# Block 0 of an attention-and-GLU kernel listed anew: eight raw buffers, own buffers for batch 0, some steps on GpSimd

## The chip, the cores and the metric

One core of one Trainium2 chip. The time is that of one execution on the device in microseconds (us); the kernel before was run three times. A profiled execution on the same kind of core gives the rows. Engines in the rows: PE is TensorE (matmul), PEld its weight loads, DVE is VectorE, ACT is ScalarE, POOL is GpSimd, SP is SyncE, whose queue issues most loads. A q behind the name (SPq) is the engine's instruction queue.

## What is computed

Attention over 8 batches, 8 heads, 576 positions and 64 columns, then a gated layer over all 4608 tokens.

```python
scores = scale * np.matmul(q, k.transpose(0, 1, 3, 2))
mask_local = (rel >= 0) & (rel < stride)                                   # heads 0 to 3, stride 32
mask_strided = (rel >= 0) & (pos[None, :] % stride == pos[:, None] % stride)  # heads 4 to 7
attn = np.exp(scores - max); attn = attn / (sum + 1e-09); x = attn @ v
gate = 1.0 / (1.0 + np.exp(-(x @ w_gate)))
out = (gate * (x @ w_val)) @ w_out         # x: 4608 x 512, w_gate and w_val: 512 x 1536, w_out: 1536 x 512
```

A query sees at most 32 keys in the local heads and 18 in the strided ones, and the kernel computes only the blocks that hold them.

## The kernel before

**Pieces.** A piece is a pair of heads of one batch, 32 in all: pieces 0 and 2 of a batch are local, 1 and 3 strided. Its steps: Q and V load queries with keys, and values (L261, L265); S scores on TensorE (L295); F masks them out of PSUM (L310, L315), takes the row maximum (L319) and subtracts it (L323), all on VectorE; E is the exponential on ScalarE (L334); N the row sum, its small corrections and the product with its reciprocal on VectorE (L338 to L344); T transposes on TensorE (L355, L359), P copies the result out on ScalarE (L376, L378); X weighs the values on TensorE (L399). The result is split in two float32r parts, high by ScalarE (H, L435) and low by VectorE (L, L439), and the last 64 tokens of the batch are kept apart (R, L448). Each piece gives one 128-row quarter of the 512-wide x of its batch.

**Blocks.** The gated layer goes over nine blocks of 512 tokens: block k is the first 512 tokens of batch k, block 8 the rests. For each of twelve f (128 columns of the hidden layer) a block has a gate product g, a value product v and an output product O or o, each of twelve 128x128x512 matmuls (three per quarter of x: high by high, high by low, low by high; L478, L509). Between them stand sigmoid s (ScalarE, L486), gating m (VectorE, L491), and the split of the hidden part, high x (ScalarE, L498) and low y (VectorE, L502). From block 3 on two blocks at a time take sums of weights out of DRAM (L762), which saves products; those sums are made on GpSimd during blocks 1 and 2 (L685, L690).

**Weights.** The 36 weights (f, i), i = 0 gate, 1 value, 2 output, are given as float64 words and turned into two float32r parts while block 0 runs. W loads 512 KB into a raw buffer (L215); a and b take the upper and the lower word out of it (ScalarE, L225 and L229); w shifts the upper word (L234) and adds the lower one as integers (L235), on VectorE; u rounds this to the upper part (ScalarE, L244); l subtracts to get the lower part (VectorE, L248). There are two raw buffers, raw0 and raw1, in turn, and three pairs of word buffers. The parts stay in SBUF, in 33 tiles w0_0 to w10_2 and some stages for f = 11.

**Order.** Each engine takes its instructions in the order in which they stand in two written lists, ORDER (block 0 with batches 0 and 1) and REST_ORDER (everything else); the queue of an engine stands still at an instruction whose operands or buffers are not ready. In ORDER the four pieces of batch 0 are spread among the first weights. Pieces 0 and 2 of batch 0 share one set of buffers (work), 1 and 3 another (first), so piece 2 loads when piece 0 has left its buffers. Loads go out on SP's queue, for batch 1 and the later values on ScalarE's. The first products of f = 0 and f = 1 go by quarters (g0.1.0 is f = 0, i = 1, first quarter), as the pieces come.

Of the kernel before, what the change touches and what calls it, by code (L numbers as in the profile page):

```python
# [20 lines left out]
P = 128  # L21
STRIDE = 32
QB = 64
# [5 lines left out]
VL = SL // 2 * LG + NBL % LG  # L29
LQK = S + STRIDE + S  # L30
# [48 lines left out]
N12 u10.1 a10.2 b10.2 l10.1 T12 W11.1 w10.2 P12 m9 u10.2 X12 l10.0 x9 l10.2 g10.1 V13 y9 R12 H12 a11.0 L12
b11.0 S13 W11.2 w11.0 u11.0 g10.0 Z13 F13 l11.0 O9 E13 a11.1 N13 s10 T13 b11.1 m10 g11.0 P13 w11.1 x10 u11.1  # L80
y10 l11.1 X13 s11 a11.2 g11.1 H13 b11.2 L13 R13 w11.2 O10 m11 u11.2 l11.2 x11 y11
"""
REST_ORDER = """
LQ0 g1.0 pa0.0.0 LV0 pb0.0.0 pl0 v1.0 s1.0 pa0.0.1 o0.11 pb0.0.1 m1.0 e0.0 x1.0 d0.0 e0.1 y1.0 d0.1 S0.0 LQ1 M0.0 M0.1 D0 g1.1 A0 U0 E0 v1.1 N0 s1.1
W0 e0.2 e0.3 g1.2 d0.2 m1.1 d0.3 B0.0 x1.1 y1.1 v1.2 B0.1 s1.2 B0.2 ph0.0.0.1 ph0.0.1.0 B0.3 o1.0 m1.2 Z1 pw0.0.0 x1.2 y1.2 pd0.0.0 pw0.0.1 X0.0
pd0.0.1 S1.0 LV1 H0 R0 L0 o1.1 LQ2 M1.0 pa0.1.0 M1.1 D1 A1 U1 pb0.1.0 g1.3 E1 N1 pa0.1.1 ph0.1.0.1 W1 v1.3 s1.3 B1.0 pb0.1.1 B1.1 o1.2 ph0.1.1.0 m1.3
B1.2 x1.3 y1.3 g1.4 B1.3 pw0.1.0 pw0.1.1 pd0.1.0 v1.4 s1.4 pd0.1.1 g1.5 m1.4 pa1.0.0 x1.4 y1.4 pb1.0.0 pl1 v1.5 s1.5 pa1.0.1 ph1.0.0.1 pw1.0.0 o1.3
m1.5 pd1.0.0 pb1.0.1 x1.5 y1.5 X1.0 ph1.0.1.0 pw1.0.1 S2.0 LV2 H1 pd1.0.1 o1.4 R1 L1 LQ3 M2.0 M2.1 D2 A2 pa1.1.0 g1.6 U2 E2 pb1.1.0 N2 v1.6 s1.6 W2
B2.0 pa1.1.1 ph1.1.0.1 B2.1 o1.5 m1.6 pb1.1.1 B2.2 x1.6 y1.6 g1.7 ph1.1.1.0 B2.3 pw1.1.0 Z3 pw1.1.1 pd1.1.0 v1.7 s1.7 pd1.1.1 g1.8 m1.7 pa2.0.0 x1.7
y1.7 pb2.0.0 pl2 v1.8 s1.8 pa2.0.1 ph2.0.0.1 pw2.0.0 o1.6 m1.8 pd2.0.0 pb2.0.1 x1.8 y1.8 X2.0 ph2.0.1.0 pw2.0.1 S3.0 LV3 H2 pd2.0.1 R2 L2 o1.7 LQ4  # L90
# [79 lines left out]
def attention_then_glu(ctx, tc, qk_l, qk_s, v_l, v_s, w_all, consts, out):  # L170
# [742 lines left out]
```

## Time and profile before

| | |
|---|---|
| median of 3 runs (lowest to highest) | 947.76 us (947.62 to 949.39) |
| profiled execution, its own time | 949.55 us |
| its span in the profile | 947.8 us |
| TensorE busy | 919.4 us (97%) |
| VectorE, ScalarE, GpSimd busy | 609.9, 429.8, 120.1 us |
| first matmul | 5.19 us |
| first output product of block 0 | 52.13 us |
| first gate product of block 1 | 151.18 us |

The profile page has the busy time of each engine, the span in 40 slices, the DMA queues, the chain of work that ended last, and the costliest groups of instructions. A row of a group names line, engine, operation, tiles out of and into which it works, its shape and number, then busy us, mean ns of one, and the idle time of the engine ahead of it with what ended it. A row by stages gives, for a stretch of the span, each engine's busy us with the number of instructions, then the granted clock of TensorE, the share of the DMA engines and GB/s. Ends of matmuls are modelled: consecutive ones overlap, so that 0.39 us stand for one while twelve take 2.72.

### The profile page before, as it was taken

The numbers are of one execution on the slowest core, as the hardware profiler recorded it, in microseconds if no ns is written. First come the engines' busy times: TensorE is split into PE (matmuls) and PEld (weight loads), VectorE is DVE, ScalarE is ACT, GpSimd is POOL, SyncE is SP. The second block draws the span as 40 slices with busy tenths as digits, with TensorE's granted clock in tenths as the row PEclk, the third lists the DMA queues.
The fourth block names the chain that finished last, engine by engine and source line by source line (L and its number), as shares of the span: only waits on it lengthen the run. The fifth ranks groups of instructions, "written<-read, shape, count | busy, mean of one in ns | idle before, by whom it ended". The sixth has DMA issues, their size and how long they took to land.

```text
span 947.8 us, 18546 instructions
## 1 busy us (share of the span) xinstructions
PE 919.4 (97%) x7624; PEld 755.6 (80%) x7624; DVE 609.9 (64%) x991; ACT 429.8 (45%) x783; POOL 120.1 (13%) x182
## 2 busy tenths in 40 slices
PE   4899899999999999999999999999999999999998
PEld 3687677888878888888888888888888888888886
DVE  6887685865689889876667887766337534333331
ACT  3786864443346445544445534444435333222221
POOL 0000002355515352100000111000002100000000
PEclk9999999999999999999999999999999999999999
DMA  6766564366547657665555525554455046444211
GB/s 239 239 183 215 158 191 143 121 207 190 176 137 226 195 172 227 203 196 188 175 186 173 172 68 186 178 188 149 138 164 164 23 136 197 150 143 152 67 45 44
DMA packets 89637, 154.15 MB, mean 163 GB/s; under 512 B 5840, under 2 KB 40016, under 8 KB 89552
## 3 DMA queue, kind: packets, MB, share of 16 engines
q1 hardware_dynamic: 87632, 146.72, 48.8%
q10 hardware_dynamic: 1920, 6.24, 2.1%
q8 instruction: 60, 0.98, 0.4%
q14 instruction: 25, 0.20, 0.1%
HBM read 121.48 MB, written 31.46 MB: 161 GB/s over the span
## 4 chain that ended last, share of the span: by engine, by line
PE 84%; DVE 6%; DMA 5%; ACT 3%; issue 1%; SPq 0%; ACTq 0%; DVEq 0%
PE p L762 21%; PE o L509 17%; PE d L762 15%; PE v L478 8%; PE g L478 7%; PE o_a L509 5%; DMA raw<-in_w_all 4%; PE x_a L399 2%; PE o_g L509 2%; PE o_v L509 2%; DVE pt L368 1%; PE s_v L295 1%; PE s_g L295 1%; PE s L295 1%; PE x L399 1%
## 5 line engine op out<-in xcount | busy, mean ns | idle before, releaser
L762 PE MATMUL p<-xs,ring 128*128 128x512 f32 x864 | 204.6, 389 | 0.0
L762 PEld LDWEIGHTS p<-xs,ring 128*128 128x128 f32 x864 | 162.2, 188 | 33.7
L509 PE MATMUL o<-w,hh 128*128 128x512 f32 x576 | 180.4, 394 | 0.0
L762 PE MATMUL d<-xs,ring 128*128 128x512 f32 x648 | 155.6, 389 | 0.0
L762 PEld LDWEIGHTS d<-xs,ring 128*128 128x128 f32 x648 | 121.6, 188 | 25.3
L509 PEld LDWEIGHTS o<-w,hh 128*128 128x128 f32 x576 | 106.3, 188 | 22.7
L509 PE MATMUL o<-w,hl 128*128 128x512 f32 x288 | 112.2, 390 | 0.0
L796 DVE TENSOR_TENSOR e<-e,d 128x512 f32<-128x512 f32 x54 | 37.1, 687 | 109.7 <-PE d L762 61.9
L368 DVE STREAM_TRANSPOSE pt<-sb 32x320 f32<-32x320 f32 (+1 forms) x192 | 102.9, 536 | 3.8
L478 PE MATMUL g<-xh,w 128*128 128x512 f32 x256 | 85.6, 393 | 1.8 <-DVE sb L310 0.6
L478 PE MATMUL v<-xh,w 128*128 128x512 f32 x256 | 86.6, 398 | 0.0
L791 ACT COPY e<-p 128x512 f32<-128x512 f32 x54 | 31.7, 587 | 114.9 <-PE p L762 114.7
L509 PEld LDWEIGHTS o<-w,hl 128*128 128x128 f32 x288 | 54.1, 188 | 11.8 <-DVE hl L502 0.3
L478 PEld LDWEIGHTS g<-xh,w 128*128 128x128 f32 x256 | 48.0, 188 | 13.0 <-ACT e L486 1.0
L478 PEld LDWEIGHTS v<-xh,w 128*128 128x128 f32 x256 | 49.1, 192 | 10.5
L690 POOL TENSOR_TENSOR sum<-sum 128x128 f32<-128x128 f32 x96 | 51.4, 535 | 7.4
L478 PE MATMUL v<-xl,w 128*128 128x512 f32 x128 | 50.7, 396 | 0.0
L478 PE MATMUL g<-xl,w 128*128 128x512 f32 x128 | 50.0, 390 | 0.4 <-DVE xl L439 0.4
L502 DVE TENSOR_TENSOR hl<-hid,hh 128x512 fp32r<-128x512 f32 x36 | 26.9, 750 | 34.3 <-ACT hh L498 34.1
L804 ACT ACTIVATE e<-e 128x512 f32<-128x512 f32 x54 | 34.2, 633 | 30.2 <-DVE e L796 30.2
L275 POOL MEMSET sb<- 128x120 f32 x16 | 3.5, 216 | 341.7 <-DVE pt L368 213.6
L685 POOL TENSOR_TENSOR sum<-w 128x256 f32<-128x256 f32 x44 | 34.7, 808 | 92.3 <-DMA sets<-sum 67.0
(122 smaller groups left out, 1399.9 us busy)
## 6 DMA issues: line engine op xcount, KB each, us to landing
ring<-sets SPq DMA_DIRECT2D x126, 512.0 KB, 4.1
raw<-in_w_all SPq DMA_DIRECT2D x36, 512.0 KB, 4.3
qk<-in_qk_s SPq DMA_DIRECT2D x14, 599.0 KB, 5.7
vv<-in_v_l SPq DMA_DIRECT2D x13, 640.0 KB, 4.6
qk<-in_qk_l SPq DMA_DIRECT2D x14, 592.0 KB, 5.2
out<-ob SPq DMA_DIRECT2D x32, 256.0 KB, 2.0
sets<-w SPq DMA_DIRECT2D x24, 256.0 KB, 4.0
sets<-sumh SPq DMA_DIRECT2D x24, 256.0 KB, 2.8
```

Of the source, the lines that this page charges most:

```text
L295: nc.tensor.matmul(sc[j % len(sc)][g * m : (g + 1) * m, j // len(sc) * BANK + s * kk : j // len(sc) * BANK + (s + 1) * kk], qk[d, q0 : q0 ...
L368: nc.vector.transpose(dst[to : to + LB, :, col : col + LB], src[part * LB : (part + 1) * LB, :, h * LB : (h + 1) * LB])
L399: nc.tensor.matmul(at_bank(r, (u * per + g) * m, (u * per + g + 1) * m)[j * D : (j + 1) * D], v[rows, (u * per + g) * P + j * D : (u * per ...
L478: nc.tensor.matmul(o, w, x, start=first and n == 0, stop=last and n == len(todo) - 1)
L502: nc.vector.tensor_tensor(hl, whole_h.pop((k, f)), hh.bitcast(F32), op=ALU.subtract)
L509: nc.tensor.matmul(acc[k][i], h[:, i * P : (i + 1) * P], w, start=f == 0 and n == 0, stop=f == NF - 1 and n == 2,)
L685: nc.gpsimd.tensor_tensor(u[:, at : at + 2], part(wh[f][i], c), part(wl[f][i], c), op=ALU.add)
L690: nc.gpsimd.tensor_tensor(u[:, to], u[:, x], u[:, y], op=op)
L762: nc.tensor.matmul(to, w[:, (wi * 2 + c) * P : (wi * 2 + c + 1) * P], x[xi][:, c], start=p in (1, 2, 5) and c == j == 0, stop=c == 1 and j ...
L791: nc.scalar.copy(x, two[m, 0])
L796: nc.vector.tensor_tensor(x, x, two[m, 1], op=ALU.add)
L804: nc.scalar.activation(x, x, AF.Sigmoid)
```

## The change

- One list, ORDER, takes the place of the two; the words of block 0 get an f ahead (fS0.1 is the scores of batch 0, piece 1) or a w (wa0.1). Its first part, up to g1.0, is in a new order; behind that TensorE's steps keep their order, and single steps of the other engines and queues change places.
- Eight raw buffers: raw0, raw1 and the six tiles of w9 and w10, until these weights themselves are made (RAWS: weight, raw buffer, word buffers). Word buffers are the three pairs s0 to s2 and, for some, w4_1, w4_2 and w5_0.
- Pieces 2 and 3 of batch 0 have buffers of their own in tiles of w5 to w8 (HOMES); their queries, keys and values are loaded by separate transfers. Piece 1 has the area first alone.
- All loads of block 0 go out on SP's queue.
- Batch 0's pieces start with piece 1, and all four are worked ahead of most weights. The gate and value products of f = 0 and 1, and of f = 2 as well, go by quarters.
- The parts F, N and w are taken apart: fM, fA, fU; fN, fW; ws (shift), wd (add). Variants on other engines, with the times that they occur ahead of g1.0: wdp, the add on GpSimd (16 of 36); wlp, the weight's lower part on GpSimd (13 of 36); wuv, the upper part on VectorE and not ScalarE (21 of 36); fUp and fWp, the subtraction of the maximum (6 of 8) and the product with the reciprocal (4 of 8) on GpSimd; xv, the hidden high part on VectorE (5 of 12); yp, the hidden low part on GpSimd (5 of 12).

The diff, cut to its core (the list to its first part):

```diff
 BANKS = {
-    "S00": "a", "S01": "o0", "T00": "o1", "X00": "a", "S02": "o1", "T01": "o0", "X01": "a", "S03": "o0", "T02": "o1", "X02": "a", "T03": "o0", "X03": "a",
+    "S0.0": "o1", "S0.1": "o1", "T0.1": "o0", "X0.1": "o0", "T0.2": "o1", "X0.2": "o1", "S0.3": "o1", "T0.3": "o0", "g1": "o0",
 }
+HOMES = {
+    2: {"q": "w7_0", "k": "w7_1", "v": "w7_2", "u": "w8_0", "sb": "w8_1", "pt": "w8_2"},
+    3: {"q": "w6_0", "k": "w6_1", "v": "w6_2", "sb": "w5_2", "pt": "w5_1"},
+}
+RAWS = """
+0.0:raw0:s0 0.1:raw1:s1 1.0:w9_0:s2 1.1:w9_1:w4_1 0.2:w9_2:w4_2 2.0:w10_0:w5_0 2.1:w10_1:s0 1.2:w10_2:s1 2.2:raw0:s2 3.0:raw1:w4_1 3.1:w9_0:w4_2
...
+"""
 ORDER = """
-C Q00 Q01 V00 W0.1 S00 Z00 F00 S01 Q03 V01 Q02 W0.0 Z01 F01 E00 a0.1 b0.1 N00 E01 w0.1 T00 P00 N01 u0.1 S02
-a0.0 X00 b0.0 l0.1 Z02 F02 W1.0 W1.1 T01 V02 R00 H00 P01 L00 E02 S03 w0.0 a1.0 N02 X01 u0.0 b1.0 g0.1.0 V03
-W0.2 Q10 w1.0 T02 H01 R01 l0.0 u1.0 Z03 F03 g0.0.0 P02 a1.1 b1.1 l1.0 a0.2 W2.0 w1.1 E03 g1.0.0 b0.2 L01 u1.1
...
+fQ0.1 fZ0.1 fZ0.3 C fQ0.0 fQ0.2 fV0.2 fQ0.3 fV0.1 wr0.1 fV0.0 wr0.0 fS0.1 fV0.3 wr2.0 wr1.0 wr1.1 wr0.2 fM0.1 wr2.1 wr1.2 fA0.1 fS0.0 fU0.1 fQ1.0
+fM0.0 fE0.1 fS0.2 fN0.1 fA0.0 fW0.1 fUp0.0 fM0.2 fT0.1 fA0.2 fE0.0 fS0.3 fUp0.2 fP0.1 fN0.0 fX0.1 fM0.3 fWp0.0 fE0.2 fA0.3 fR0.1 fH0.1 fN0.2 wa0.1
+fUp0.3 fT0.0 wb0.1 fW0.2 wr3.0 fP0.0 fL0.1 fT0.2 fE0.3 ws0.1 wa0.0 fN0.3 wdp0.1 fX0.0 fP0.2 wb0.0 fW0.3 wu0.1 wr2.2 fX0.2 fV1.0 ws0.0 fR0.0 fH0.0
+wlp0.1 wd0.0 wa2.0 fT0.3 fL0.0 fH0.2 wb2.0 wuv0.0 wl0.0 fR0.2 wr4.1 fg0.1.0 fP0.3 ws2.0 fg0.0.0 fL0.2 wa1.0 wdp2.0 wb1.0 fX0.3 ws1.0 wa1.1 wd1.0 wr3.1
+wuv2.0 fg0.1.1 fH0.3 ws1.1 wlp2.0 wu1.0 fg0.0.1 fL0.3 wb1.1 fg0.1.2 wl1.0 fR0.3 wr3.2 wb0.2 fg0.0.2 wd1.1 wa0.2 fg1.0.0 wuv1.1 wa2.1 wr4.0 fg0.0.3
...
     def load_weight(f, i):
-        at = order.index((f, i)) % 2
-        raws[f, i] = stage(f"raw{at}", f"raw{f}_{i}").rearrange("p (n t) -> p n t", t=2)
-        nc.sync.dma_start(raws[f, i], w_all[f, :, i, :, :])
+        at, name = homes[f"{f}.{i}"][0], f"raw{f}_{i}"
+        t = stage(at, name) if at[0] == "r" else pool.tile([P, 2 * DM], I32, tag=at, name=name)
+        raws[f, i] = [t.rearrange("p (n t) -> p n t", t=2), 2]
+        nc.sync.dma_start(raws[f, i][0], w_all[f, :, i, :, :])
...
+    def shift(f, i):
+        high = words[f, i][0]
+        nc.vector.tensor_scalar(high, high, 3, None, op0=ALU.logical_shift_left)
+
+    def whole(f, i, by=nc.vector):
         high, low = words[f, i]
-        nc.vector.tensor_scalar(high, high, 3, None, op0=ALU.logical_shift_left)
-        nc.vector.tensor_tensor(high, high, low, op=ALU.add)
+        by.tensor_tensor(high, high, low, op=ALU.add)
+
+    def upper(f, i, by=nc.scalar.copy):
+        weight_tile(f, i)
+        by(wh[f][i], words[f, i][0].bitcast(F32))
+
+    def lower(f, i, by=nc.vector):
+        by.tensor_tensor(wl[f][i], words.pop((f, i))[0].bitcast(F32), wh[f][i].bitcast(F32), op=ALU.subtract)
...
-        def load_qk(queue=nc.sync):
-            tiles["qk"] = qk = space.tile([P, SQK], F32, tag="qk", name=f"qk{b}_{step}")
-            queue.dma_start(qk[:, :cols], (qk_l if local else qk_s)[b, p])
+        def load_qk():
+            if home:
+                for n, lo, hi in (("q", 0, at_k), ("k", at_k, cols)):
+                    tiles[n] = pool.tile([P, hi - lo], F32, tag=home[n], name=f"{n}{b}_{step}")
+                    nc.sync.dma_start(tiles[n], (qk_l if local else qk_s)[b, p, :, lo:hi])
+                return
+            qk = space.tile([P, SQK], F32, tag="qk", name=f"qk{b}_{step}")
+            nc.sync.dma_start(qk[:, :cols], (qk_l if local else qk_s)[b, p])
...
-        def soft_sub():
+        def soft_sub(by=nc.vector):
             prob, _, by_row = rows()
-            nc.vector.tensor_tensor(prob, prob, by_row, op=ALU.subtract)
+            by.tensor_tensor(prob, prob, by_row, op=ALU.subtract)
...
+        fUp=lambda b, p: firsts[b, p]["U"](nc.gpsimd), fWp=lambda b, p: firsts[b, p]["NW"](nc.gpsimd), fg=first_products,
+        wr=load_weight, wa=upper_words, wb=lower_words, ws=shift, wd=whole, wdp=lambda f, i: whole(f, i, nc.gpsimd), wu=upper,
+        wuv=lambda f, i: upper(f, i, nc.vector.tensor_copy), wl=lower, wlp=lambda f, i: lower(f, i, nc.gpsimd),
+        xv=lambda k, f: split_high_h(k, f, nc.vector.tensor_copy), yp=lambda k, f: split_low_h(k, f, nc.gpsimd),
```

More of the change, by code (lines that the diff above doesn't have):

```diff
@@ L246, in lower, with word @@
-    def lower(f, i):
-        a, _ = words.pop((f, i))
-        nc.vector.tensor_tensor(wl[f][i], a.bitcast(F32), wh[f][i].bitcast(F32), op=ALU.subtract)
+        at, name = homes[f"{f}.{i}"][0], f"raw{f}_{i}"
+        t = stage(at, name) if at[0] == "r" else pool.tile([P, 2 * DM], I32, tag=at, name=name)
+        raws[f, i] = [t.rearrange("p (n t) -> p n t", t=2), 2]
+        nc.sync.dma_start(raws[f, i][0], w_all[f, :, i, :, :])
+    def word(f, i, half):
+        t, left = raws[f, i]
+        raws[f, i][1] = left - 1
+        if left == 1:
+            raws.pop((f, i))
+        else:
+            at, name = homes[f"{f}.{i}"][1], f"{f}_{i}"
+            if at[0] == "s":
+                words[f, i] = stage("h" + at[1:], "high" + name), stage("l" + at[1:], "low" + name)
+            else:
+                both = pool.tile([P, 2, DM], I32, tag=at, name="words" + name)
+                words[f, i] = both[:, 0], both[:, 1]
+        return t[:, :, half]
@@ L362, in turn_blocks @@
         def turn_blocks(part):
-            if part == 0:
+            if "pt" not in tiles:
                 tiles["pt"] = space.tile([P, 2 * SS * QB], F32, tag="pt", name=f"pt{b}_{step}")
@@ L371, in spread @@
             tp = todo["spread"]
-            tiles["pt"] = pt = space.tile([P, 2 * SS * QB], F32, tag="pt", name=f"pt{b}_{step}")
+            tiles["pt"] = pt = attn_tile("pt", f"pt{b}_{step}")
             n = len(pairs) * P
@@ L550, in glu_out @@
             give_out(k, NTT - 1, slice(DM // 2, DM), nc.vector.tensor_copy)
-    for f in range(LATE):
-        weight_tiles(f)
     ps = ctx.enter_context(tc.tile_pool(name="ps", bufs=1, space=bass.MemoryType.PSUM))
@@ L561, in attention_then_glu @@
     left_over(0)
-    firsts = {(b, p): pair(b, p, first if b == 0 and p % 2 else work) for b in range(2) for p in range(4)}
+    firsts = {(b, p): pair(b, p, first if b == 0 and p == 1 else work) for b in range(2) for p in range(4)}
     products_of = {}
-    def step(what):
-        kind, of = what[0], what[1:]
-        if kind in "QVZSFENTPXHLR":
-            b, p = int(of[0]), int(of[1])
-            args = ()
-            if kind in "QV":
-                args = (nc.sync if b == 0 and (kind == "Q" or p < 2) else nc.scalar,)
-            elif kind in "STX":
-                args = (bank(BANKS.get(what, "a"), f"{kind.lower()}{b}_{p}"),)
-            firsts[b, p][kind](*args)
-        elif kind == "C":
-            nc.sync.dma_start(cst, consts)
-        elif kind in "Wabwul":
-            dict(W=load_weight, a=upper_words, b=lower_words, w=whole, u=upper, l=lower)[kind](*map(int, of.split(".")))
-        elif kind == "g":
-            f, i, c = (map(int, of.split("."))) if of.count(".") == 2 else (*map(int, of.split(".")), None)
-            if c in (0, None):
-                if f == 1:
-                    if i == 0:
-                        products_of[1, "both"] = bank("o1", "gv0_1")
-                    o = products_of[1, "both"][:, i * BANK : (i + 1) * BANK]
-                else:
-                    o = ps.tile([P, BANK], F32, tag="gv"[i], name=f"{'gv'[i]}0_{f}")
-                products_of[f, i] = o
-            if c is None:
-                products(products_of[f, i], 0, f, i)
-            else:
-                products(products_of[f, i], 0, f, i, cs=((0, 2, 1, 3)[c],), first=c == 0, last=c == 3)
-        elif kind == "s":
-            sigmoid(0, int(of), products_of[int(of), 0])
-        elif kind == "m":
-            gated(0, int(of), products_of[int(of), 1])
-        elif kind in "xy":
-            dict(x=split_high_h, y=split_low_h)[kind](0, int(of))
-        elif kind == "O":
-            glu_out(0, int(of))
@@ L603, in attention_then_glu, with in_bank @@
-    with tc.manual_schedule():
-        for what in ORDER.split():
-            step(what)
-            if what == "X03":
-                first_area.close()
-                odd = ctx.enter_context(tc.tile_pool(name="odd", bufs=1))
-                x_tiles(1)
-                left_over(1)
-    first_banks.close()
-    ps_b = ctx.enter_context(tc.tile_pool(name="ps_b", bufs=1, space=bass.MemoryType.PSUM))
+    def in_bank(kind, b, p):
+        firsts[b, p][kind](bank(BANKS.get(f"{kind}{b}.{p}", "a"), f"{kind.lower()}{b}_{p}"))
@@ new lines, in first_products @@
+    def first_products(f, i, c=None):
+        if c in (0, None):
+            both = BANKS.get(f"g{f}")
+            if both and (0, f, 1 - i) not in products_of:
+                t = bank(both, f"gv0_{f}")
+                for n in range(2):
+                    products_of[0, f, n] = t[:, n * BANK : (n + 1) * BANK]
+            elif not both:
+                products_of[0, f, i] = ps.tile([P, BANK], F32, tag="gv"[i], name=f"{'gv'[i]}0_{f}")
+        o = products_of[0, f, i]
+        if c is None:
+            products(o, 0, f, i)
+        else:
+            products(o, 0, f, i, cs=((0, 2, 1, 3)[c],), first=c == 0, last=c == 3)
```

319 lines of the change are left out of this document (176 added, 143 removed).

## The prediction, on record ahead of the result

> **What bounds the kernel now.** I read first the busy time by stages, cut where the program's own order has its marks: the first output product of block 0 at 52.1 us and the first gate product of block 1 at 151.2 us.
>
> ```profile
> core 0: us, PE busy (x) PEld busy (x) DVE busy (x) ACT busy (x) POOL busy (x), PEclk, DMA share, GB/s
> 0.00:52.10 52.10, 35.55 (x584) 27.99 (x585) 38.14 (x70) 30.74 (x65) 0.60 (x6) 1.00 0.68 230
> 52.10:151.20 99.10, 94.31 (x862) 75.81 (x861) 78.61 (x139) 72.77 (x132) 1.03 (x3) 0.98 0.59 186
> 151.20:947.80 796.60, 789.55 (x6181) 651.77 (x6179) 493.16 (x783) 326.30 (x587) 118.50 (x174) 1.00 0.49 155
> ```
>
> After 151.2 us TensorE idles for 7.0 of 796.6 us, and the change leaves its order there untouched: read off the two lists, the 446 TensorE steps behind this mark follow each other as before. What can be won or lost lies ahead of it. Next the timeline of TensorE (start, duration, line, tiles, and in brackets the idle time before) and one step of the chain of waits, for the price of its work and for the marks.
>
> ```profile
> 5.19 1.41 PE L295 MATMUL s<-qk 64*32 64x64 f32 x80 [5.19 <-DMA qk<-in_qk_l]
> 8.51 1.55 PE L295 MATMUL s<-qk 64*64 64x54 f32 x48 [1.92 <-DMA qk<-in_qk_s]
> 52.13 0.61 PE L509 MATMUL o<-w,hh 128*128 128x512 f32 x2
> 54.94 1.04 PE L295 MATMUL s<-qk 64*32 64x64 f32 x80
> 66.97 0.60 PE L355 MATMUL t<-cst,sb 128*128 128x128 f32 x4
> 67.50 0.30 PE L359 MATMUL t<-cst,sb 64*64 64x64 f32 x2
> 78.83 1.49 PE L399 MATMUL x<-pt,vv 64*64 64x32 f32 x72
> 100.88 0.84 PE L355 MATMUL t<-cst,sb 128*128 128x128 f32 x6 [2.15 <-DVE sb L344]
> 134.51 0.92 PE L295 MATMUL s<-qk 64*64 64x54 f32 x48
> 144.77 0.91 PE L399 MATMUL x<-pt,vv 54*64 54x54 f32 x44
> 151.18 0.39 PE L478 MATMUL g<-xh,w 128*128 128x512 f32 x1
> ```
>
> ```profile
> 111.09 2.72 PE g L478 x12
> ```
>
> A product step of twelve matmuls takes 2.72 us; a local piece 1.04 + 0.60 + 0.30 + 1.49 = 3.43, a strided one 0.92 + 0.84 + 0.91 = 2.67. Ahead of 151.2 stand 35 products (12 gate, 12 value, 11 output) and four pieces of each kind: 95.2 + 13.7 + 10.7 = 119.6 us. So 31.6 us are lost. Ahead of 52.1 stand six products' worth (two weights' blocks of f = 0 and of 1, and f = 2) and batch 0's four pieces: 16.3 + 12.2 = 28.5, so 23.6 are lost there and 8.0 behind. Then who kept the others waiting: the waits of the load queue, the groups of ScalarE and VectorE up to 151.2 us, and the later subtractions that GpSimd does (least, median and most ns).
>
> ```profile
> SPq L215 <- ACT low L229: 68.8, 32, 5.3
> ```
>
> ```profile
> L225 ACT ACTIVATE high<-raw 128x512 f32<-128x512 f32 x36 | 24.2, 671 | 20.3 <-DMA raw<-in_w_all 18.5 <-PE s L295 0.8 <-DVE w L248 0.7
> L244 ACT CAST w<-high 128x512 fp32r<-128x512 f32 x34 | 20.8, 617 | 2.2 <-DVE high L235 2.0 <-issue 0.2
> L235 DVE CUSTOM_DVE_ANT_0 high<-high,low 128x1024 uint16<-128x1024 uint16 x36 | 24.9, 692 | 4.7
> L248 DVE TENSOR_TENSOR w<-high,w 128x512 fp32r<-128x512 f32 x34 | 23.2, 687 | 7.8 <-ACT w L244 7.6
> L234 DVE TENSOR_SCALAR high<-high 128x512 int32<-128x512 int32 x36 | 15.2, 421 | 1.4 <-ACT high L225 1.3
> L323 DVE TENSOR_TENSOR sb<-sb,mx 128x640 f32<-128x640 f32 x4 | 3.3, 824 | 0.1
> L502 DVE TENSOR_TENSOR hl<-t,hh 128x512 fp32r<-128x512 f32 x12 | 8.2, 686 | 0.3 <-ACT hh L498 0.3
> ```
>
> ```profile
> L736 POOL TENSOR_TENSOR xd<-xraw x6: 1296/1456/1674, 370.4 to 736.4; 128x512 f32<-128x512 f32 x6
> ```
>
> With two raw buffers the load queue stood 68.8 us for ScalarE to give one back, and ScalarE in turn 18.5 us for the load that had been held up. VectorE works 116.7 of 151.2 us (38.1 + 78.6), ScalarE 103.5, GpSimd 1.6.
>
> **The change, part by part.** *Loads.* Eight raw buffers take the queue's wait for ScalarE off the first eight weights, and all loads of batch 0 go out at the start. What runs then is bandwidth:
>
> ```profile
> 4.00:6.00 2.00, 0.81 (x60) 0.81 (x65) 0.00 (x0) 0.00 (x0) 0.00 (x0) 1.00 0.95 373
> 8.00:10.00 2.00, 1.49 (x48) 1.37 (x48) 1.13 (x2) 0.74 (x1) 0.00 (x0) 1.00 0.47 192
> ```
>
> Full queues move 373 GB/s, half-empty ones 192. Batch 0, the constants and eight weights are some 9 MB: 24 us at the full rate, landing by about 27. The last of these weights is wanted by ScalarE only behind some 25 us of its own work, so I cost the early loads at nothing; without the cover (at 192 GB/s) they would end at 49 and cost 10 us and more. The strided piece goes first, without constants and local queries ahead of it: 0.6 MB instead of 0.86, 0.7 us less at 373 GB/s, so VectorE starts near 6.0 and not 6.6. Nine loads move from ScalarE's queue to SP's; a load held there by a buffer (batch 1's values behind batch 0's) holds the weights behind it. SP has eight weights of lead, so I take nothing for that.
>
> *VectorE.* It gives GpSimd 16 integer adds (0.692), 13 lower parts of weights (0.687), 5 of hidden (0.686) and 10 softmax steps (0.82): 11.1 + 8.9 + 3.4 + 8.2 = 31.6 us. It takes from ScalarE 21 upper parts of weights and 5 of hidden. No VectorE copy from SBUF to SBUF is in the trace; the shift (0.42) is the nearest row below, the subtraction (0.69) above: 10.9 to 17.9, I take 14.4, the middle, and 3.5 either way into the range. Sum: 116.7 - 31.6 + 14.4 = 99.5. *ScalarE* loses 26 casts of 0.617: 103.5 - 16.0 = 87.5. Neither is then the bound by its sum alone.
>
> *GpSimd* gets 44 steps. One of 128x512 takes 1.30 when undisturbed (the least of the row), one of 640 by width 1.6: 34 x 1.3 + 10 x 1.6 = 60 us of 151, which it has. An integer add and a broadcast operand are not in its rows; if they cost twice, 21 + 16 more, which still fits its queue but not what follows.
>
> *Two engines at one door.* GpSimd's steps are not free to VectorE:
>
> ```profile
> 348.12 1.75 POOL L736 TENSOR_TENSOR xd<-xraw,xraw 128x512 f32<-128x512 f32 x1
> 349.50 0.39 DVE L339 TENSOR_SCALAR mx<-mx 128x10 f32<-128x10 f32 x1
> 571.07 1.70 POOL L736 TENSOR_TENSOR xd<-xraw,xd 128x512 f32<-128x512 f32 x1 [0.83 <-DVE xs L748]
> 571.53 1.91 DVE L323 TENSOR_TENSOR sb<-sb,mx 128x640 f32<-128x640 f32 x1
> ```
>
> ```profile
> L339 DVE TENSOR_SCALAR mx<-mx 128x10 f32<-128x10 f32 x4 | 0.7, 174 | 0.1
> ```
>
> The subtraction took 1.91 in place of 0.82: it ended 0.67 after GpSimd's step, so it stood until that was almost through. A scalar step of 0.174 took 0.39 and ended with GpSimd's (349.87). So a GpSimd step can hold up VectorE by 0 to 1.1 us, according to what VectorE has next. Masks (from PSUM) and maxima are not seen to wait; shifts, adds and subtractions, some two thirds of VectorE's work here, may. With GpSimd at work two fifths of the time I take 0.4 us a step: 44 x 0.4 = 18.
>
> The Trainium skill ("SBUF — State Buffer", Who interferes with whom) states this as a rule that speaks against the change: a VectorE instruction with two SBUF inputs and a GpSimd one that reads SBUF exclude each other for the whole instruction. The two rows above agree; taken as complete exclusion, it leads to the slower rival below.
>
> *First stretch.* VectorE's queue ahead of the first output step holds 5 masks, 5 maxima, 2 subtractions, 4 sums with their two small steps, 3 products, 4 low parts of x, 9 shifts, 6 adds, 5 copies, 5 lower parts and 3 hidden steps, about 36.8 us by the rows, against 38.1 that it worked before. From 6.0 that ends at 42.8. Before it idled 7.4 us here beside the start (52.1 - 6.6 - 38.1); with four pieces in buffers of their own and the weights landed I leave 2. GpSimd has 12 steps: 12 x 0.4 = 4.8, of which 3 on the path (some fall into the waits). First output step near 48, with TensorE's 28.9 us done (quarter products differ): 4.5 us gained with what it has done more.
>
> *Second stretch.* TensorE has 119.6 - 28.9 = 90.7 us left, VectorE 99.5 - 36.8 = 62.7 and 32 x 0.4 = 12.8: TensorE bounds, with less room than these sums show, since adds and lower parts come in bunches. Of the 8.0 us lost before (the stall of 2.15 us above is its largest) I leave 4. Block 1 begins at 48 + 90.7 + 4 = 142.7 and not at 151.2: 8.5 us less.
>
> *The rest* is reordered on VectorE, ScalarE and the queues by single places; TensorE is covered (7.0 us idle, over half in the tail): nothing, 1 us either way.
>
> Span 947.8 - 8.5 = 939.3. The profiled execution took 949.55, 1.75 more than its span, and stands 1.8 above the median of 947.76; against the median the same difference gives 939.3.
>
> **The rivals.** *Faster.* If GpSimd's steps fall into VectorE's waits and maxima, the first stretch loses no 3 us and the second no 4 but 2: 5 us more, block 1 at 137.7, 934.3. For it: VectorE idled 28 us in all before (151.2 - 6.6 - 116.7). Against: the two rows of waiting.
>
> *No gain.* VectorE's waits stay: 6.0 + 99.5 + 28 + 18 = 151.5, block 1 where it was, 947.8 to 948.1. For it: chains of four engines run in order, each with its queue, and a step that goes through GpSimd takes 1.3 where it took 0.69. Against: 18.5 us of ScalarE's waits had the two raw buffers as cause.
>
> *Slower.* Exclusion in full: VectorE's waits shrink to 15, but each step holds it for b. It then ends at 6.0 + 99.5 + 15 + 44 b, and from b = 0.70 on that is later than 151.2. At b = 0.9, near a whole step of 1.3 less its edges, it is 160.1, and 956.7. Steps that cost twice on GpSimd (integer add, broadcast) lead here too. Against: the mean over GpSimd's long steps in the trace is smaller, as maxima and PSUM operands pass.
>
> **How the numbers follow.** Forecast 0.52, faster rival 0.17, no gain 0.14, slower 0.17. A difference of 0.2% (1.9 us) is about what a measurement of this kernel can tell from none. Faster is the forecast and its rival, 0.69; same, the no-gain case, 0.14; slower, 0.17. The range goes from the faster rival to just above no gain, 933.5 to 949; the forecast alone has 935.8 to 942.8 (3.5 for the copies).
>
> **What would show it.** Right: ScalarE's wait for raw loads falls from 18.5 to under 6; the first output step lies at 46 to 50 and block 1's first gate product at 139 to 146; behind it TensorE idles 7 us as before; the groups of VectorE that read two SBUF operands rise above 0.69 (to 0.8 or 0.9) while masks and maxima stay. Wrong: GpSimd's steps far above 1.3 to 1.7, VectorE nearly full with means above 1.0, or a first output step later than 52.

## The result: slower by 0.7%, and where the time went

The changed kernel takes 955.32 us (median of 8 runs, 955.12 to 957.52), the kernel before, run beside it, 948.58 (8 runs, 946.08 to 953.29): a ratio of 1.0071 (95% interval 1.0049 to 1.0094). The forecast was 939.3 with a range up to 949.0. The profiled execution took 955.16 with a span of 953.4, 5.6 more than the 947.8 of before.

The stages of the changed kernel, cut at the same marks as before (first output product, block 1's first gate product):

```profile
core 0: us, PE busy (x) PEld busy (x) DVE busy (x) ACT busy (x) POOL busy (x), PEclk, DMA share, GB/s
0.00:46.21 46.21, 35.88 (x662) 30.21 (x663) 36.06 (x63) 28.17 (x59) 15.68 (x17) 1.00 0.92 341
46.21:147.18 100.97, 95.29 (x784) 75.14 (x783) 82.53 (x128) 63.84 (x114) 51.82 (x45) 0.98 0.43 136
147.18:953.40 806.22, 798.53 (x6181) 652.29 (x6179) 489.99 (x783) 326.62 (x587) 113.15 (x166) 1.00 0.49 155
```

The first stretch is 5.9 us shorter than before (46.2 for 52.1), the second 1.9 longer (101.0 for 99.1), and the rest, where nothing was expected, 9.6 longer (806.2 for 796.6). Of that, TensorE's busy time is 9.0 (798.5 for 789.5), its idle time 0.6. So TensorE was not kept waiting there: its own steps became longer. The chain of waits shows which (start, us, step with its matmuls):

```profile
147.34 2.79 PE g L512 x12
150.13 2.80 PE v L512 x12
152.93 2.80 PE o L543 x12
...
247.78 2.72 PE v L512 x12
250.50 2.80 PE o L543 x12
```

Before, each of these took 2.72. Now gate and value products of block 1 and the output products of every block take 2.80; the gate and value products of block 2 (at 247.78) take 2.72 still. The split is by operand tiles: all output products read the hidden tiles, and block 1's gate and value products the second x tiles. The change has one more line, which the core of the diff above doesn't show:

```diff
-            tiles["mx"] = space.tile([P, 16], F32, tag="mx", name=f"mx{b}_{step}")
+            tiles["mx"] = space.tile([P, 16], F32, tag="mx" + str(step) * bool(home), name=f"mx{b}_{step}")
```

The two pieces with homes of their own thereby get two small tiles of their own, 16 x 4 = 64 bytes each per partition, in work. Everything that is laid out behind them in work and odd (hidden parts, second x tiles, word buffers) stands 128 bytes further on in SBUF, and the weights don't. Modulo 256, weights and hidden tiles stood at the same place before, and stand 128 apart now. These places are worked out from the sizes and the order of the tiles; no profile shows an address.

Ahead of block 1, TensorE's timeline has the two marks and its waits of over 0.4 us:

```profile
46.21 0.64 PE L543 MATMUL o<-w,hh 128*128 128x512 f32 x2
...
58.67 0.47 PE L512 MATMUL v<-xh,w 128*128 128x512 f32 x1 [2.44 <-DVE t L525]
...
82.32 0.50 PE L512 MATMUL g<-xh,w 128*128 128x512 f32 x1 [0.45 <-ACT e L520]
...
91.04 0.47 PE L512 MATMUL v<-xh,w 128*128 128x512 f32 x1 [2.15 <-ACT w L260]
...
131.94 0.47 PE L512 MATMUL g<-xh,h 128*128 128x512 f32 x1 [0.64 <-DVE h L260]
...
147.18 0.40 PE L512 MATMUL g<-xh,w 128*128 128x512 f32 x1
```

The groups of ScalarE, VectorE and GpSimd up to 147.18 us that answer to those shown of before:

```profile
L244 ACT ACTIVATE high<-raw 128x512 f32<-128x512 f32 x30 | 20.0, 673 | 13.2 <-DVE l L263 4.8 <-DMA raw<-in_w_all 4.7 <-DVE w L263 3.2
L256 DVE CUSTOM_DVE_ANT_0 high<-high,low 128x1024 uint16<-128x1024 uint16 x18 | 18.2, 1013 | 0.9
L252 DVE TENSOR_SCALAR high<-high 128x512 int32<-128x512 int32 x30 | 17.4, 591 | 3.4 <-ACT high L244 3.4
L263 DVE TENSOR_TENSOR w<-high,w 128x512 fp32r<-128x512 f32 x18 | 17.4, 973 | 1.4 <-ACT w L260 1.1
L256 POOL TENSOR_TENSOR high<-high,low 128x512 int32<-128x512 int32 x12 | 16.0, 1340 | 18.5 <-DVE high L252 11.7 <-ACT low L248 6.7
L263 POOL TENSOR_TENSOR w<-high,w 128x512 fp32r<-128x512 f32 x10 | 14.3, 1433 | 12.5 <-DVE w L260 6.6 <-ACT w L260 4.7 <-DVE high L252 1.3
L260 DVE CAST w<-high 128x512 fp32r<-128x512 f32 x16 | 7.6, 477 | 2.7 <-POOL high L256 2.4
L353 DVE TENSOR_REDUCE mx<-sb 128x10 f32<-128x640 f32 x4 | 3.2, 805 | 0.1
```

The maxima of before, for the last of these rows:

```profile
L319 DVE TENSOR_REDUCE mx<-sb 128x10 f32<-128x640 f32 x4 | 3.3, 821 | 0.1
```

ScalarE's wait for raw loads fell from 18.5 to 4.7 us in this row, and to 6.4 in all (the reading of the lower words, L248, waits 1.7 for them, and waited for none before); the load queue's wait for ScalarE (68.8 before):

```profile
SPq L223 <- ACT low L248: 30.8, 12, 7.7
```

VectorE's steps on the weights, whose operands all lie in SBUF, grew: the add from 0.69 to 1.01, the subtraction from 0.69 to 0.97, the shift from 0.42 to 0.59. The maxima, which read SBUF too, stayed (0.82 before, 0.81 now).

### The profile page after: what moved, and what is told of

The parts are those of the page before. It is cut to its first block, busy times and chain, and to the rows that moved or that the text cites. A ratio compares the mean times of both kernels' runs of the same rounds, so it can differ in the third digit from the quotient of the medians.

```text
span 953.4 us, 18540 instructions
## 1 busy us (share of the span) xinstructions
PE 929.7 (98%) x7624; PEld 757.6 (79%) x7624; DVE 608.6 (64%) x973; ACT 418.6 (44%) x759; POOL 180.7 (19%) x226
## 4 chain that ended last, share of the span: by engine, by line
PE 85%; DVE 8%; DMA 2%; ACT 2%; SPq 1%; issue 1%; POOL 1%; DVEq 0%; ACTq 0%
PE p L770 21%; PE o L543 18%; PE d L770 15%; PE g L512 7%; PE v L512 7%; PE o_a L543 5%; PE o_g L543 3%; PE o_v L543 3%; PE x_a L433 2%; DVE high L256 1%; DVE w L263 1%; PE s_g L329 1%; PE s_v L329 1%; PE s L329 1%; PE x L433 1%
## 5 line engine op out<-in xcount | busy, mean ns | idle before, releaser
L543 PE MATMUL o<-w,hh 128*128 128x512 f32 x576 | 183.4, 399 | 0.0
L512 PEld LDWEIGHTS g<-xh,w 128*128 128x128 f32 x256 | 48.0, 188 | 15.5 <-DVE sb L349 1.8
L536 DVE TENSOR_TENSOR hl<-hid,hh 128x512 fp32r<-128x512 f32 x36 | 28.0, 780 | 36.5 <-ACT hh L532 36.4
L532 ACT CAST hh<-hid 128x512 fp32r<-128x512 f32 x36 | 22.3, 620 | 53.0 <-PE o_a L543 43.6
```

Of the source, the lines that this page charges most:

```text
L512: nc.tensor.matmul(o, w, x, start=first and n == 0, stop=last and n == len(todo) - 1)
L536: by.tensor_tensor(hl, whole_h.pop((k, f)), hh.bitcast(F32), op=ALU.subtract)
L543: nc.tensor.matmul(acc[k][i], h[:, i * P : (i + 1) * P], w, start=f == 0 and n == 0, stop=f == NF - 1 and n == 2,)
```

## The experiments

My theory at this point: the 9.6 us behind block 1's mark are the operands' distance, and GpSimd's steps are worth little since they hold VectorE up. Rivals: the steps are longer for another reason (the order, the loads beside them, an engine at the same memory), or the distance counts only together with the new order; and GpSimd's steps are a gain all the same. The kernel before spreads by 8 us from execution to execution (945.7 to 953.9 in 34 runs beside the first four experiments, median 950.04), so spans and marks of the profiles count beside the medians.

**Small tiles of 128 bytes (e1_mx256).** The changed kernel; what lies behind the tiles moves on by 128 more, to a distance of 256.

```diff
-tiles["mx"] = space.tile([P, 16], ...)
+tiles["mx"] = space.tile([P, 32 if home else 16], ...)
```

> The changed kernel with the two new 64-byte tiles mx2 and mx3 made 128 bytes each, so that every tile behind them lies 256 bytes later than before the change and not 128; list and engines as they are. Address theory (the product steps of 2.80 us come from two operands whose addresses lie 128 apart modulo 256): output steps back to 2.72 us all through, block 1 begins at 145 to 148 us as in the changed kernel, behind it 797 us as in the kernel before and not 806; span near 944, time near 945.7, faster than before by 0.2 to 0.4%. Rival (the new order of the other engines, or GpSimd's work, slows the products): steps stay at 2.80, span 953, time 955.

948.90 us (12 runs, 947.00 to 949.68), ratio 0.9989 (0.9973 to 1.0005): 6.4 under the changed kernel. The chain and the rest behind block 1:

```profile
147.79 2.72 PE g L512 x12
```

```profile
147.63:946.60 798.97, 790.94 (x6181) 651.61 (x6179) 490.75 (x783) 326.43 (x587) 114.96 (x167) 1.00 0.49 156
```

The steps are back at 2.72, and the rest takes 799.0 for 806.2. So 7.2 of the 9.6 us are the distance; 2.4 are not, and they are most of what this version stays above the time expected of it.

**The kernel before, one tile 128 bytes larger (e2_before_128).** Nothing of the change is in it.

```diff
-tiles["mx"] = space.tile([P, 16], ...)
+tiles["mx"] = space.tile([P, 48 if space is work else 16], ...)
```

> The kernel before with its mx tile of the common buffers 128 bytes larger, nothing else: hidden parts and the odd blocks' x lie 128 bytes later, weights and the even blocks' x where they were. Address theory: output steps 2.80 us in every block, gate and value steps 2.80 in block 1 and 2.72 in blocks 0 and 2; 108 output and 24 other steps by 0.08 are 10.5 us, so span near 958. Rival (order or engines): 2.72, 947.8.

955.67 us (9 runs, 952.93 to 959.84), ratio 1.0070 (1.0049 to 1.0091): the same loss as the whole change, from one unused stretch of memory.

```profile
167.87 2.80 PE o L509 x12
...
175.65 2.78 PE g L478 x12
```

```profile
146.33:951.20 804.87, 797.65 (x6181) 652.29 (x6179) 492.44 (x783) 326.12 (x587) 118.06 (x174) 1.00 0.49 154
```

804.9 for 796.6. The order has no part in it. The span of the profile (951.2) is 6.8 lower than expected: block 1 began at 146.33 in it and not at 151.18, and the loss behind the mark is 8.3 and not some 10. In four profiles of the kernel before and its shifted versions (e3 and e11 below) this mark lies between 146.3 and 154.3.

**Everything moved by 128 (e3_before_all128).** The kernel before with an unused tile ahead of all others.

```diff
+    pad = pool.tile([P, 32], F32, name="pad")
     cst = pool.tile([P, SL * KL + GS + P], F32, name="cst")
```

> The kernel before with an unused 128-byte tile ahead of all tiles: every operand lies 128 bytes later, none in relation to another. If the distance of the two operands counts: 2.72 us everywhere, 947.8. If an operand's own place modulo 256 counts (224 slow, 96 fast): all steps 2.80, some 290 to 300 steps by 0.08, span near 971. Order or engines: 947.8.

947.00 us (10 runs, 945.32 to 951.54), ratio 0.9975 (0.9955 to 0.9995): a little under the kernel before, within its spread; nothing here explains the 0.25%.

```profile
152.80 2.72 PE g L479 x12
...
158.24 2.72 PE o L510 x12
```

No step is longer. So it is the distance between the two operands that counts and not the place of either. Why it counts stays open.

**64 bytes (e11_before_64).** As e2, with a tile larger by 64 bytes (32 columns for 48).

> The kernel before with one small tile 64 bytes larger, so that the hidden and odd tiles stand 64 bytes off the weights' place modulo 256 (128 in the slow versions, 0 in the kernel before). If only a distance of 128 is slow, an output step takes 2.72 us as before and the time is 946 to 953. If every distance but 0 is slow, it takes 2.80, and the time is 953 to 959. A value between (2.74 to 2.78) would say that the loss grows with the distance.

One execution: 960.14 us, above the range expected, since block 1 began as late as 154.31 in it.

```profile
151.67 2.80 PE o L509 x12
154.47 2.76 PE g L478 x12
...
175.60 2.80 PE o L509 x12
```

The output product takes 2.80 at 64 bytes as at 128; some gate products take a little less. With 0 and 256 it takes 2.72. Other distances weren't tried.

**No step on GpSimd (e4_no_gpsimd).** e1 with all 44 steps of block 0 back on VectorE, at their places in the list.

```diff
-... wdp0.1 ... wlp0.1 ... fUp0.0 ... fWp0.0 ... yp0.0 ...
+... wd0.1 ... wl0.1 ... fU0.0 ... fW0.0 ... y0.0 ...
```

> The kernel of e1 with all 44 steps of block 0 that were on GpSimd back on VectorE, at their places in the list; same results. Theory (GpSimd's steps hold VectorE by some 0.45 us each but spare it 0.72): VectorE has 12 us more to do in block 0, its stretch from 50 to 100 us is full as before, block 1 begins 5 to 10 us later, at 151 to 157 us; span 949 to 954. Rival (the holding costs as much as it spares, or chains through GpSimd are what is late): block 1 at 147 us or earlier, span 944 or less.

945.75 us (10 runs, 944.87 to 946.70), ratio 0.9957 (0.9939 to 0.9975). The rival was right: 3.2 us faster than e1, which is the same kernel with GpSimd's help. Block 1 begins at 145.15 (147.63 in e1). VectorE's groups, undisturbed:

```profile
L256 DVE CUSTOM_DVE_ANT_0 high<-high,low 128x1024 uint16<-128x1024 uint16 x30 | 20.3, 686 | 0.7
L263 DVE TENSOR_TENSOR w<-high,w 128x512 fp32r<-128x512 f32 x28 | 18.9, 685 | 0.9 <-ACT w L260 0.7
L252 DVE TENSOR_SCALAR high<-high 128x512 int32<-128x512 int32 x30 | 12.4, 422 | 2.6 <-ACT high L244 2.4
L260 DVE CAST w<-high 128x512 fp32r<-128x512 f32 x16 | 6.7, 416 | 0.3
```

These four rows against those of the changed kernel give the hold: 18 x (1.013 - 0.686) + 18 x (0.973 - 0.685) + 30 x (0.591 - 0.422) + 16 x (0.477 - 0.416) = 17.1 us; with the smaller groups (copies of the hidden part, 0.84 for 0.43, words, scalar steps) 23. GpSimd took 31.5 us of work off VectorE (34 steps of 0.69, 10 of 0.82), and three quarters of it came back as waiting, 0.53 us for each of the 44 steps.

**Which of GpSimd's steps (e5_adds_back, e6_low_parts_back, e10_additions_only).** e1 with one kind or two back on VectorE.

```diff
e5:  -wdp +wd                    (GpSimd keeps 28: lower parts and softmax)
e6:  -wlp -yp +wl +y             (GpSimd keeps 26: additions and softmax)
e10: -wlp -yp -fUp -fWp +wl +y +fU +fW   (GpSimd keeps the 16 additions)
```

> The changed kernel with the 256-byte tiles (948.9 us) and only the 16 integer additions of block 0 back on VectorE; 28 steps stay on GpSimd. With all 44 back the time fell by 3.15 us. If every step costs alike (it holds VectorE), 16 of 44 give back 1.1: 947.8. If the harm is the length of a chain, and a step harms by how near it stands to TensorE's products, the additions (three steps ahead of a product) cost nothing and it stays at 948.9. If they are the whole harm, 945.8.

> The same with only the 18 lower parts (13 of weights, 5 of hidden) back on VectorE, 26 steps left on GpSimd. Alike: 18 of 44 give back 1.3, 947.6. Chain: these are the last step ahead of a product, so they carry the whole harm: 945.8. If the additions or the softmax carry it: 948.9.

> The version with additions and softmax steps on GpSimd (943.84 us), with the 10 softmax steps back on VectorE too, so that GpSimd has the 16 integer additions alone. If the softmax steps, two of which follow each other within a piece, make the chain of the pieces longer (1.5 us on GpSimd in place of 0.82), their return gives 1 us: 943. If VectorE's load counts, it has 8.2 us more work and some 5 us less hold, 3 us net, and loses up to that: 944.5 to 946 (945.75 is the version with nothing on GpSimd).

e5: 948.44 us (10 runs, 947.87 to 949.14), ratio 0.9991 (0.9972 to 1.0010). e6: 943.84 (10 runs, 943.11 to 946.35), ratio 0.9935 (0.9912 to 0.9958). e10: 946.53 (10 runs, 944.04 to 947.37), ratio 0.9959 (0.9940 to 0.9978). The lower parts carry all of the harm that shows: taking them off GpSimd gives 5.1 us, taking the additions off gives 0.5, which is within the noise. One place of the timelines shows how it can happen. VectorE and GpSimd in the changed kernel, ahead of the wait of 2.44 us:

```profile
55.71 1.76 DVE L256 CUSTOM_DVE_ANT_0 high<-high,low 128x1024 uint16<-128x1024 uint16 x1
57.51 0.43 DVE L260 CAST w<-high 128x512 fp32r<-128x512 f32 x1
57.85 0.68 DVE L525 TENSOR_TENSOR t<-e,v 128x512 f32<-128x512 f32 x1
```

```profile
55.33 1.59 POOL L263 TENSOR_TENSOR w<-high,w 128x512 fp32r<-128x512 f32 x1
```

and VectorE in e6 at the same place:

```profile
55.52 0.68 DVE L256 CUSTOM_DVE_ANT_0 high<-high,low 128x1024 uint16<-128x1024 uint16 x1
56.23 0.43 DVE L260 CAST w<-high 128x512 fp32r<-128x512 f32 x1
56.58 0.68 DVE L263 TENSOR_TENSOR w<-high,w 128x512 fp32r<-128x512 f32 x1
57.18 0.68 DVE L525 TENSOR_TENSOR t<-e,v 128x512 f32<-128x512 f32 x1
```

In the changed kernel the addition stands until GpSimd's subtraction is through (55.33 + 1.59 = 56.92) and takes 1.76: 1.08 more. In e6 VectorE does the subtraction itself, which takes 0.6 of its queue, and comes to the gating, for which TensorE stands, 0.67 earlier, though it has done one step more. That this is the way in which all 18 do harm is argued from this place; that they do the harm is shown. What the additions and the softmax steps are worth isn't settled: the versions without lower parts on GpSimd (e4, e6, e10, and e9, e12 below) lie between 943.8 and 946.5, with 2 to 3 us between executions of each. The 2.7 between e6 and e10 is no price of the softmax steps either: the executions of each fall into two groups (e6 seven at 943.1 to 944.0 and three at 945.8 to 946.4, e10 four at 944.0 to 944.5 and six at 946.5 to 947.4), and the two medians come from different groups. Group by group the difference is under 1 us.

**Two raw buffers (e7_two_raw).** e4 with two raw buffers, each load listed behind the last reading of the load two ahead of it.

```diff
-0.0:raw0:s0 0.1:raw1:s1 1.0:w9_0:s2 1.1:w9_1:w4_1 0.2:w9_2:w4_2 2.0:w10_0:w5_0 ...
+0.1:raw0:s1 0.0:raw1:s0 2.0:raw0:w5_0 1.0:raw1:s2 1.1:raw0:w4_1 0.2:raw1:w4_2 ...
```

> The version without GpSimd steps (945.75 us) with two raw buffers in place of eight; each load stands in the list behind the last reading of the load two ahead of it, in the order in which the words are taken. All else stays: own buffers for the pieces of batch 0, copies on VectorE, the list. If the raw buffers are what moved block 1 from 151 to 145 us, it goes back by 3 to 6 us, to 949 to 952, and the executions spread over several us as those of the kernel before do (945.7 to 953.9). If the pieces' own buffers and the order did it, it stays within 1 us of 945.75.

961.26 us (4 runs, 961.06 to 961.78), ratio 1.0129 (1.0086 to 1.0172), block 1 at 160.83: 15.5 us lost, three times what was expected. ScalarE's waits for raw loads:

```profile
ACT low L241 <- DMA raw<-in_w_all: 20.1, 10, 5.6
ACT high L237 <- DMA raw<-in_w_all: 11.3, 4, 3.9
ACT words L237 <- DMA raw<-in_w_all: 5.1, 2, 3.2
```

36.5 us, where the kernel before had 18.5: the new list lives on early loads. The guess that two raw buffers alone make the spread of the kernel before fails: these four executions lie within 0.7 us. Where that spread comes from stays open.

**Copies back on ScalarE (e8_copies_back).** e4 with the upper parts that VectorE copies back on ScalarE.

```diff
-... wuv0.0 ... xv0.1 ...
+... wu0.0 ... x0.1 ...
```

> The version without GpSimd steps (945.75 us) with the upper parts (of weights and of hidden) that VectorE copies in block 0 back on ScalarE. VectorE worked 48.06 of the 50 us from 50 to 100 us, ScalarE 38.05. If VectorE's load bounds that stretch, its 26 copies of about 0.45 us are 11.7 us less for it and TensorE's stalls there (0.62 and 2.16 us) go: 943 to 944.5. If ScalarE's order is what counts (its queue holds the casts to words and the sigmoids too, and 26 times 0.617 is 16 us more for it), no gain or up to 3 us slower: 945.7 to 949.

947.99 us (10 runs, 946.59 to 949.08), ratio 0.9992 (0.9971 to 1.0014): 2.2 slower than e4. The copies on VectorE are a gain, and the rival was right: ahead of block 1, the copies on ScalarE add 13.2 us to its work (105.6 for 92.3) and take 9.1 off VectorE's (113.4 for 122.5).

**The rest in the order of before (e9_rest_of_before).** e6, with the list behind block 1's first gate product as REST_ORDER had it.

```diff
-g1.0 v1.0 s1.0 o0.11 m1.0 x1.0 e0.0 y1.0 d0.0 e0.1 S0.0 ...
+g1.0 v1.0 s1.0 o0.11 m1.0 e0.0 x1.0 d0.0 e0.1 y1.0 d0.1 S0.0 ...
```

> The version with additions and softmax steps on GpSimd and the lower parts on VectorE (943.84 us; block 1 at 145.0, 799.5 behind it), with the order of all steps behind block 1's first gate product as the kernel before has it. Behind that mark the versions of the changed kernel without the address effect take 798.9 to 799.5 us, the kernel before 796.6 and its shifted version 797.2. If the reordering of the rest costs these 2.4 us (1.0 of idle TensorE, the rest in steps that take longer): 941.4, and 797 behind the mark. If they come from what block 0 leaves (buffers, addresses, the place of loads in flight), it stays at 943.8.

944.00 us (7 runs, 941.38 to 944.73), ratio 0.9933 (0.9909 to 0.9958). The median is that of e6; behind the mark the two profiles differ, e6 first, then e9:

```profile
145.01:944.50 799.49, 790.96 (x6181) 651.66 (x6179) 492.17 (x783) 326.78 (x587) 112.72 (x164) 1.00 0.49 156
```

```profile
145.67:942.90 797.23, 790.52 (x6181) 651.76 (x6179) 493.41 (x783) 326.46 (x587) 113.39 (x164) 1.00 0.50 156
```

797.2 as expected (797), 2.3 less, most of it idle time of TensorE (6.7 for 8.5). The lowest and the highest execution are 1.7 and 1.6 under those of e6; the medians hide this, as the executions of both fall into two groups. The other profiles agree: without the distance, the six versions with the new order of the rest (e1, e4, e5, e6, e8, e10) take 798.9 to 799.5 behind the mark, and the four with the order of before (the kernel before, e3, e9, e12) 796.6 to 797.5. So the new order of the rest cost some 2 us.

**Softmax alone on GpSimd (e12_softmax_only).** e9 with the additions back on VectorE as well.

> The version with additions and softmax steps on GpSimd, the lower parts on VectorE and the rest in the order of before (944.0 us), with the 16 integer additions back on VectorE too: GpSimd has the 10 softmax steps alone. The softmax steps were worth 2.7 us (946.53 without them, 943.84 with them). If the additions are worth nothing (16 times 0.69 saved on VectorE, about 9 us of it given back as hold, and 1.4 in place of 0.69 in a weight's chain; 948.44 without them and 948.9 with them beside the lower parts), this is 943 to 944. If they unload VectorE where it bounds (48.5 of 50 us busy from 50 to 100 us), their return costs up to 2 us: 944.5 to 946.

943.81 us (12 runs, 942.82 to 944.52), beside a kernel before of 948.43 (17 runs): ratio 0.9953 (0.9935 to 0.9970). The additions are worth nothing that shows. e6, e9 and e12 are the fastest versions, 0.5 to 0.7% under the kernel before; e4 and e10 are 0.4% under it. No version with nothing on GpSimd had the rest in the order of before. By the 2 us that this order is worth, e4 would stand near 943.7, an estimate, where e9 and e12 stand: no gain from any step on GpSimd is shown.

## Why the prediction was wrong, step by step

The forecast's span was 939.3 and the changed kernel's is 953.4, 14.1 more. By its own terms: first output product 46.2 for 48, 1.8 better; second stretch 101.0 for 94.7, 6.3 worse; the rest 806.2 for 796.6, 9.6 worse. 9.6 + 6.3 - 1.8 = 14.1.

**The rest: the step that failed.** "Nothing, 1 us either way", because TensorE's order is the same and TensorE is covered. The order is the same and the idle time is (7.7 for 7.0, as the text had it). But the price of a step was taken for a constant of the shape. Where a tile lies is a part of the change, and a new tag lays the tiles out anew: 7.2 us by e1, 8.3 by e2 in the kernel before. The reordering by single places cost 2.3 more (e9), outside the 1 us that was allowed. With the distance alone gone the kernel takes 948.9 (e1), no gain against before.

**Loads.** Right in direction: ScalarE's wait for raw loads is 4.7 in the row that the prediction went by (L244; under 6 was the mark) and 6.4 with L248, and 341 GB/s run in the first stretch. For the loads without their cover the prediction had 10 us and more; without the eight buffers the new list loses 15.5 us (e7).

**VectorE, ScalarE, GpSimd.** GpSimd's 44 steps take 62 us for 60; the integer addition takes 1.34 to 1.40 and not twice as much. The copies take 0.42 undisturbed (e4), the lower end of what was taken (0.42 to 0.69). VectorE's busy time up to block 1 is 118.6, for 99.5 + 18 of hold = 117.5: the sum holds by luck, as two misses nearly cancel: the hold was 23 us and not 18 (0.53 a step and not 0.4), and the 26 copies cost 3.5 less than the 14.4 taken. ScalarE worked 92.0 us for 87.5; that wasn't followed up.

**Two engines at one door.** The size came near (0.53 us a step for 0.4); what it was worth was not asked. A hold of 0.53 a step against 0.69 saved leaves VectorE 0.16 a step, and for that a step takes 1.4 in place of 0.69 in its chain. The prediction subtracted the saved time in one place and added the hold in another, and never set the one against the other by kind of step: for the lower parts, the last step ahead of TensorE's products, the balance is negative (e6, 5.1 us). The rows of waiting agree with the rule that the prediction cited (the Trainium skill, "SBUF — State Buffer", Who interferes with whom), and with its finer points, which the prediction left out: the shift and the copies, with one SBUF input, are held too (0.42 to 0.59, and 0.42 to 0.48 for those of the weights), as the page says of scalar steps and copies in their two-port modes, while maxima stay (0.81), as it says of reductions. One of the two rows that the prediction rested the rule on, the scalar step of 0.39, has one input and belongs here too.

**First stretch.** 46.2, within the 46 to 50 given, again with misses that cancel: VectorE worked 36.1 us in it, hold and all, where the sum had 36.8 and 3 of hold, and stood some 3.9 us behind its start at 6.2, where the sum left 2.

**Second stretch.** "TensorE bounds, 4 us lost" was wrong: 101.0 - 90.7 = 10.3 were lost. The timeline has 5.7 us of waits (2.44, 0.45, 2.15, 0.64); eleven output products at 2.80 are 0.9; and behind the wait of 2.44 us the granted clock fell to half:

```profile
56.00:58.00 2.00, 0.24 (x2) 0.00 (x0) 1.97 (x3) 1.07 (x3) 0.93 (x1) 1.00 0.79 211
58.00:60.00 2.00, 1.33 (x5) 1.16 (x6) 1.44 (x4) 1.38 (x3) 1.05 (x1) 0.91 0.75 197
60.00:62.00 2.00, 2.00 (x6) 1.52 (x6) 2.00 (x2) 1.45 (x3) 2.00 (x2) 0.50 0.44 141
62.00:64.00 2.00, 2.00 (x52) 1.29 (x50) 1.79 (x4) 0.70 (x1) 0.05 (x1) 0.74 0.71 242
```

2 x (0.09 + 0.50 + 0.26) = 1.7 us more. The remaining 2.0 were not taken apart. e10 shows the same stretch without a clock loss:

```profile
47.92:143.85 95.93, 92.42 (x785) 74.18 (x783) 84.48 (x147) 63.90 (x114) 25.14 (x26) 1.00 0.45 143
```

95.9 us, near the 94.7 of the forecast, and block 1 at 143.85, within the 139 to 146 given for it. So the length forecast for the second stretch was reached in a version that differs from the change in three things: the operands' distance is gone, lower parts and softmax steps are back on VectorE, and no wait is over 2 us. What each is worth in this stretch alone isn't shown.

**The rivals.** "Slower" ended on the right side by another road: its mechanism, a hold of 0.70 or more a step, wasn't reached (0.53). The operands' distance was in none of the rivals.

## What to carry to other kernels

When a change adds, drops or renames a tile, compare the places of the operands of the bounding engine before and after it, and price one step of each kind again; a step that has grown in every block points to the layout and not to the order. Set what a helper engine saves against what it holds up, step by step by kind, and don't give it the last step ahead of the bounding engine. Whether steps with slack behind them are a gain isn't shown here; they did no harm that shows. A wait of TensorE of some 2 us can cost nearly as much again in granted clock (1.7 us here).

## What the runs showed of the hardware

A product step of twelve 128x128x512 float32r matmuls takes 2.72 us when stationary and moving operand stand at the same place modulo 256 bytes in a partition, and 2.80 when they stand 64 or 128 apart (some 6 ns a matmul, 7 to 8 us over this kernel). The distances are those worked out from the tiles' sizes, and 0, 64, 128 and 256 are all that ran. The Trainium skill ("SBUF — State Buffer", Who interferes with whom) gives the two operands ports of their own, called independent; by these runs their addresses aren't independent in time.

With single waits of TensorE of 2.12 to 2.54 us ahead of block 1 (the changed kernel, e1, e4, e5, e6, e9, e12) the granted clock fell to 0.50, late in the wait or within 2 us behind it, as in the rows above; their losses add up to 3.4 us at half speed, 1.7 us of time, each (twice that in e12). Behind waits of 1.54 (e5, e8) and 1.81 (e10) it stayed at 1.00, and behind the 2.15 at 91.04 of the changed kernel too: near 2.1 us it goes either way. In e7 it fell to 0.50 even behind a wait of 1.94 (at 42.19, with shorter ones of 0.54 and 0.19 in the 8 us before), so the length of the wait alone doesn't decide. The Trainium skill ("TensorE: Matmul & The Clock Gate", Why this matters for your kernels) puts the gap that matters above some 3 us; here less was enough, and the measurement decides.
